# Pooled softmax scalars in PSUM, all SBUF splits on GpSimd, a first pass of 320 tokens and a new order table, in a fused attention and feed-forward kernel

## The chip, the cores and the metric

One core of a Trainium2 chip runs the whole program. The metric is device time in microseconds of one execution. The engines are TensorE (PE, with its weight loads as PEld), VectorE (DVE), ScalarE (ACT), GpSimd (POOL) and SyncE (SP), whose queue issues nearly all DMAs.

## The reference

Eight batches of eight heads, 576 positions, head size 64. Attention is the sum of two parts: a pooled softmax over means of four positions, repeated four times, and a softmax over a band of seven neighbours. The result goes through a feed-forward layer.

```python
q_d = q.reshape(B, H, Sd, factor, D).mean(axis=3)      # the same for k, v
out_d = sm_attn(q_d, k_d, v_d)
out_up = np.repeat(out_d, factor, axis=2)
mask = np.abs(pos[:, None] - pos[None, :]) < factor
scores = np.where(mask, scale * q @ k^T, -1e9)
out_local = softmax(scores) @ v
x = (out_up + out_local).transpose(0, 2, 1, 3).reshape(B * S, H * D)   # 4608 x 512
h = x @ w_in                                            # w_in 512 x 2048
out = np.maximum(0.01 * h, h) @ w_out                   # w_out 2048 x 512
```

## The kernel before

**Feed-forward.** The 4608 tokens are cut into twelve chunks: the first batch into 256 and 320 tokens, the other seven batches into ten chunks of 256 to 512 (`plan`). A float32 factor is held as a high part (rounded to the fp32r type) and a low part (the rest), and each product is three matmuls: high by high, high by low, low by high. `w_in` and `w_out` are cut into 16 blocks f. Of each chunk the up-projection makes one PSUM bank per f (line 1169, 12 matmuls), `leaky` (lines 1259 to 1263) applies the activation on ScalarE twice and takes the low part `gl` on VectorE, and the down-projection adds it to four accumulator banks (line 1298, 12 matmuls for each f). The passes are: chunk 0 over f 0 to 7, chunk 1 over all f, chunk 0 over f 8 to 15, and then the other chunks.

**Weights** come in 64-bit floats and are joined to float32 in `convert`: a cast on ScalarE (line 405), a join on VectorE (407), the high part on VectorE or ScalarE (420, 424), the low part on GpSimd (427). In the first pass this goes on while TensorE already multiplies.

**Fast products.** The last four chunks have 512 tokens and use seven products in place of eight half-size ones for two blocks f (`products`, line 1199). Their seven operands T0 to T6 are sums of the quarters of x and come from `operands`: `split` copies an operand's high part on ScalarE (504) and takes its low part (507), on GpSimd for T1 and T5 and on VectorE for the other five; `less` (514) makes the sums on VectorE. x lies in SBUF (`stage`, `hmem`), the sums in PSUM (`pt`).

**Attention.** Batch 0 goes through TensorE: `pooled`, and `banded` in windows of 64 queries, in two stretches (`BLKS`), one for chunk 0 and one for chunk 1. For batches 1 to 7, GpSimd multiplies (lines 990 and 1054), VectorE sums (997, 1061), and TensorE only transposes; the pooled part runs in `pair`, twice for each batch, 14 times in all. A `pair` scores on TensorE into two banks (line 779), takes the maxima on VectorE into a small SBUF tile `st` (785), scales them there (787), lets ScalarE exponentiate and sum into `st` (793), turns the sums into factors (798, 800, VectorE) and multiplies by them (805, ScalarE).

```python
nc.vector.tensor_scalar(out=st[:, :, 0], in0=st[:, :, 0], scalar1=-SCALE / (FAC * FAC), ...)   # 787
nc.vector.tensor_scalar(out=rc, in0=rc, scalar1=1e-9, scalar2=float(FAC), ...)                 # 798, rc = st[:, :, 1]
(nc.vector if eng == "DVE" else nc.gpsimd).tensor_tensor(out=lo, in0=x, in1=hi..., op=subtract) # 507
```

**Order.** Every engine runs its instructions in the order in which the program has issued them. `Order.run` sets it: each task (a `pair`, a weight, a chunk) has a rank, and the instruction that could start first by a table of costs goes next, ties by rank. `SHIFTS` moves the ranks of single tasks. The banks are eight: two `hp` for the up-projection, four accumulators, and `pt0` and `pt1`, which all the rest shares.

Of the kernel before, what the change touches and what calls it, by code (L numbers as in the profile page):

```python
# [13 lines left out]
ALU = mybir.AluOpType  # L14
AX = mybir.AxisListType
PSUM = bass.MemoryType.PSUM

B, H, S, D = 8, 8, 576, 64
DE = D + 1
FAC = 4  # L20
SD = S // FAC
# [11 lines left out]
FSPLIT = 8  # L33
BANDED = 1
WIN = 64 + W - 1
BLKS = ((0, 4), (4, 9))
HALFS = 4
HEADS = 2
HF = NF // 2
# [4 lines left out]
HN = 256  # L44
# [2 lines left out]

def plan():

    chunks, at = [(0, 256, ()), (256, 320, ())], S  # L50
    parts = {b: [] for b in range(BANDED, B)}
    g = 0
    for i, n in enumerate(SIZES):
        mine, z = [], g + n
        while g < z:
            b, j = divmod(g, BLK)
            room = min(BLK - j, z - g)
            m = -(-room // -(-room // MAXSEG))
            mine.append((b + BANDED, j, j + m, (g - z + n) * NBLK))
            parts[b + BANDED].append((i + 2, j, j + m, (g - z + n) * NBLK))  # L60
            g += m
        chunks.append((at, n * NBLK, tuple(mine)))
        at += n * NBLK
    assert g == (B - BANDED) * BLK
    return chunks, parts
# [6 lines left out]
def pieces(j0, j1):  # L72
# [13 lines left out]
RATE = 270e3  # L86
SAFE = 0.4
SHIFTS = {
# [23 lines left out]
}  # L112
POLICIES = [SHIFTS]
HP, PT = ("hp0", "hp1"), ("pt0", "pt1")
# [166 lines left out]
def attn_moe(policy, ctx, tc, qkt, vd, vs3, qkb, vb, vwb, band, identb, w_in, w_out, ident, out, sums):  # L281
# [207 lines left out]
    def operands(i):  # L489
        tx = yield from wait(("x", i), LANDED[i])  # L490
        (b11, t1), (b21, b22) = ([x[:, :, :HN], x[:, :, HN:]] for x in xt[i])

        def taken(s):
            if i == FIRST:
                t = yield from wait(("up", LAST[2])) if s == 6 else wait(("emptied", bank_of(s)))
            h = yield from slot(f"t{s}")
            if i == FIRST:
                h.t = t
            return h

        def split(s, h, x, t, own=True):
            hi, lo = put(i, s)
            t = yield from op("ACT", 2 * HN, t, h.t)
            nc.scalar.copy(out=hi, in_=x)
            eng = "POOL" if s in (1, 5) else "DVE"
            t = yield from op(eng, 2 * HN, t, port=own)
            (nc.vector if eng == "DVE" else nc.gpsimd).tensor_tensor(out=lo, in0=x, in1=hi.bitcast(F32), op=ALU.subtract)
            od.signal(("T", i, s), t)
            ready[i, s] = h
            return t  # L510

        def less(out, x, y, *after, port=False):
            t = yield from op("DVE", 2 * HN, *after, port=port)
            nc.vector.tensor_tensor(out=out, in0=x, in1=y, op=ALU.subtract)
            return t

        h = yield from taken(0)
        yield from split(0, h, b11, tx)
        s_2, s_3 = yield from two(*PT)
        h = yield from taken(2)  # L520
        yield from split(2, h, t1, tx)
        t2 = bank(s_2).rearrange("p (c m) -> p c m", c=2)
        t = yield from less(t2, b22, t1, tx, s_2.t, port=True)
        h = yield from taken(3)
        tv = yield from split(3, h, t2, t, False)
        t3 = bank(s_3).rearrange("p (c m) -> p c m", c=2)
        tt = yield from less(t3, t2, b11, t, s_3.t)
        h = yield from taken(1)
        yield from split(1, h, b21, tx)
        h = yield from taken(4)  # L530
        s_3.free((yield from split(4, h, t3, tt, False)))
        h = yield from taken(5)
        tb = yield from split(5, h, b22, tx)
        t = yield from less(t2, b21, t2, tv, tt)
        h = yield from taken(6)
        t = yield from split(6, h, t2, t, False)
        s_2.free(t)
        return max(t, tb)
# [204 lines left out]
    def pair(b, u):  # L743
# [36 lines left out]
                                     qk_d[i][rows, SD:2 * SD], start=True, stop=True)  # L780
        for s in s_qds:
            s.free(t)
        for p in range(2):
            t = yield from op("DVE", 432, t, s_st.t)
            nc.vector.tensor_reduce(out=st[:, p, 0], in_=scs[p][:, :3 * SD].rearrange("p (a s) -> p a s", a=3), axis=AX.X, op=ALU.max)
        t = yield from op("DVE", 6, t)
        nc.vector.tensor_scalar(out=st[:, :, 0], in0=st[:, :, 0], scalar1=-SCALE / (FAC * FAC), scalar2=None, op0=ALU.mult)  # L787
        for p in range(2):
            t = yield from op("ACT", 432, t, s_pd.t, times=8)
            sc = scs[p]  # L790
            for qi in range(3):
                o = pds[:, qi, :, p, :QB]
                nc.scalar.activation(out=o, in_=like(sc[:, qi * SD:(qi + 1) * SD], o), func=AF.Exp, scale=SCALE / (FAC * FAC),
                                     bias=st[:, p, 0, qi:qi + 1], accum_out=st[:, p, 1, qi:qi + 1])
            s_bs[p].free(t)
        t = yield from op("DVE", 6, t)
        rc = st[:, :, 1]
        nc.vector.tensor_scalar(out=rc, in0=rc, scalar1=1e-9, scalar2=float(FAC), op0=ALU.add, op1=ALU.mult)  # L798
        t = yield from op("DVE", 6, t)
        nc.vector.reciprocal(out=rc, in_=rc)  # L800
        ts = [t, t]
# [670 lines left out]
```

## Time and profile before

| what | value |
|---|---|
| median of 3 runs | 923.71 us (922.93 to 927.31) |
| the profiled execution's own time | 923.97 us |
| its span in the profile | 921.8 us (2.1 us lie around it) |
| TensorE busy | 891.0 us, 97% of the span |
| weight loads | 827.5 us, 90% |
| VectorE, GpSimd, ScalarE | 664.1, 590.2 and 472.3 us (72%, 64%, 51%) |
| granted TensorE clock, mean | 0.991 |
| the chain that ended last | TensorE 84%, VectorE 7%, DMA 4%, ScalarE 2% |

Busy time is the time in which an engine has an instruction running. The chain that ended last is followed back from the last instruction, at each step to what released it. TensorE is the engine that is nearly always at work, so time is found where it is not: at the start, in a few gaps, at the end, and where its clock is granted at half.

### The profile page before, as it was taken

To read this page: it belongs to the slowest core of one execution; us is meant where nothing else is said; L and a number is where in the kernel's file an instruction comes from. 1 tells how busy PE (TensorE), PEld (TensorE's weight loads), DVE (VectorE), ACT (ScalarE), POOL (GpSimd) and SP (SyncE) were. 2 spreads that over 40 slices of the span, in tenths; PEclk is the share of its full clock that TensorE was granted. 3 is DMA by queue.
4 is the path that set the end of the run, shared out by engine and by line. 5 is a ranking of instruction groups with operands and counts; after the bars stand their busy time and mean duration, and the time that the engine had idled before them with its cause. 6 is when DMAs were issued, how large, how long until landed. Compare 5 with 4: busy or idle time off the path is not lost.

```text
span 921.8 us, 17665 instructions
## 1 busy us (share of the span) xinstructions
PE 891.0 (97%) x6549; PEld 827.5 (90%) x6549; DVE 664.1 (72%) x1027; ACT 472.3 (51%) x1443; POOL 590.2 (64%) x301
## 2 busy tenths in 40 slices
PE   5889999999999999999999999999999999999998
PEld 3778999999999989999999998888898888989986
DVE  5777799779788987887978789787866776232221
ACT  4668465454546446556445355554745464335332
POOL 4565887888878675847898887877676786000000
PEclk9799999999999999999999999999999999999999
DMA  9788646655435644756645627576675464315321
GB/s 256 251 262 306 211 138 210 189 163 190 158 111 180 224 133 136 268 171 198 184 159 192 224 85 265 194 268 221 206 268 193 153 218 165 125 58 160 116 92 46
DMA packets 70069, 169.21 MB, mean 184 GB/s; under 512 B 7952, under 2 KB 21008, under 8 KB 69984
## 3 DMA queue, kind: packets, MB, share of 16 engines
q1 hardware_dynamic: 69840, 167.96, 55.7%
q8 instruction: 51, 0.84, 0.4%
q14 instruction: 34, 0.28, 0.1%
q10 hardware_dynamic: 144, 0.13, 0.0%
HBM read 149.71 MB, written 18.35 MB: 182 GB/s over the span
## 4 chain that ended last, share of the span: by engine, by line
PE 84%; DVE 7%; DMA 4%; ACT 2%; issue 1%; POOL 1%; SPq 0%; POOLq 0%; DVEq 0%; ACTq 0%
PE acc L1298 39%; PE hp L1169 23%; PE hp L1199 8%; PE pt L1199 7%; PE pt L1100 1%; PE pt L826 1%; PE pt L812 1%; PE pt L779 1%; DMA prod<-in_w_out_dram 1%; DVE xloc L1061 1%; DMA v<-in_vb_dram 1%; DVE st_p L798 1%; DVE gl L1263 1%; DMA r<-sums 1%; DVE st_p L787 1%
## 5 line engine op out<-in xcount | busy, mean ns | idle before, releaser
L1054 POOL TENSOR_TENSOR prod<-v,s 128x896 f32<-128x896 f32 (+2 forms) x104 | 264.2, 2543 | 50.6 <-DVE xloc L1061 29.1
L990 POOL TENSOR_TENSOR prod<-k 128x910 f32<-128x910 f32 (+2 forms) x104 | 250.4, 2411 | 67.8 <-DVE s L997 49.7
L1298 PE MATMUL acc<-gh,w 128*128 128x320 f32 (+3 forms) x704 | 193.0, 336 | 0.0
L1259 ACT ACTIVATE gh<-hp 128x320 fp32r<-128x320 f32 (+3 forms) x155 | 72.4, 467 | 135.3 <-PE acc L1298 116.2
L1061 DVE TENSOR_REDUCE xloc<-prod 128x128 f32<-128x896 f32 (+2 forms) x104 | 132.4, 1273 | 6.6 <-POOL prod L1054 6.6
L997 DVE TENSOR_REDUCE s<-prod 128x14 f32<-128x910 f32 (+2 forms) x104 | 133.9, 1288 | 3.1 <-POOL prod L990 3.0
L1298 PEld LDWEIGHTS acc<-gh,w 128*128 128x128 f32 x704 | 124.9, 189 | 7.5 <-issue 0.8
L1169 PE MATMUL hp<-xh,w 128*128 128x320 f32 (+2 forms) x512 | 125.5, 316 | 3.2 <-DVE gl L1263 3.2
L1298 PE MATMUL acc<-gh,woh 128*128 128x320 f32 (+3 forms) x352 | 118.8, 337 | 0.0
L1298 PE MATMUL acc<-gl,w 128*128 128x320 f32 (+3 forms) x352 | 117.3, 333 | 1.1 <-DVE gl L1263 1.1
L1298 PE MATMUL acc<-gl,woh 128*128 128x320 f32 (+3 forms) x352 | 117.0, 332 | 0.8 <-DVE gl L1263 0.7
L1298 PE MATMUL acc<-gh,wol 128*128 128x320 f32 (+3 forms) x352 | 116.9, 332 | 0.0
L1263 DVE TENSOR_TENSOR gl<-hp,gh 128x320 fp32r<-128x320 f32 (+3 forms) x155 | 80.4, 519 | 45.9 <-ACT hp L1260 45.1
L1169 PEld LDWEIGHTS hp<-xh,w 128*128 128x128 f32 x512 | 89.1, 189 | 5.1 <-DVE gl L1263 4.0
L1169 PE MATMUL hp<-xl,w 128*128 128x320 f32 (+2 forms) x256 | 79.5, 311 | 0.0
L1260 ACT ACTIVATE hp<-hp 128x320 f32<-128x320 f32 (+3 forms) x165 | 77.5, 470 | 0.3
L1298 PEld LDWEIGHTS acc<-gh,wol 128*128 128x128 f32 x352 | 66.1, 188 | 4.4
L1298 PEld LDWEIGHTS acc<-gl,w 128*128 128x128 f32 x352 | 66.5, 189 | 3.9 <-DVE gl L1263 1.4
L1298 PEld LDWEIGHTS acc<-gh,woh 128*128 128x128 f32 x352 | 66.2, 188 | 2.7 <-issue 1.0
L1298 PEld LDWEIGHTS acc<-gl,woh 128*128 128x128 f32 x352 | 66.2, 188 | 2.4 <-DVE gl L1263 1.2
L1169 PE MATMUL hp<-xh,w_even 128*128 128x320 f32 (+2 forms) x256 | 65.6, 322 | 0.9 <-DVE gl L1263 0.9
L1169 PEld LDWEIGHTS hp<-xl,w 128*128 128x128 f32 x256 | 48.5, 189 | 0.0
(300 smaller groups left out, 1855.3 us busy)
## 6 DMA issues: line engine op xcount, KB each, us to landing
r<-sums SPq DMA_DIRECT2D x64, 512.0 KB, 3.5
k<-in_qkb_dram SPq DMA_DIRECT2D x48, 390.0 KB, 3.7
qk<-in_qkt_dram SPq DMA_DIRECT2D x32, 576.0 KB, 5.3
k<-in_qkb_dram SPq DMA_DIRECT2D x52, 325.0 KB, 4.7
v<-in_vb_dram SPq DMA_DIRECT2D x48, 288.0 KB, 3.4
v<-in_vb_dram SPq DMA_DIRECT2D x52, 256.0 KB, 3.6
qk<-in_vs_dram SPq DMA_DIRECT2D x28, 384.0 KB, 4.2
out_dram<-o SPq DMA_DIRECT2D x37, 128.0 KB, 3.8
```

The costliest lines, as they stand in the source:

```text
L779: nc.tensor.matmul(scs[p][outs, qi * SD:(qi + 1) * SD], qk_d[i][rows, qi * QB:qi * QB + 64], qk_d[i][rows, SD:2 * SD], start=True, stop=True)
L787: nc.vector.tensor_scalar(out=st[:, :, 0], in0=st[:, :, 0], scalar1=-SCALE / (FAC * FAC), scalar2=None, op0=ALU.mult)
L990: nc.gpsimd.tensor_tensor(out=prv, in0=view(half(s_k), 0, [[DE, nj], [1, DE]]).unsqueeze(2).to_broadcast([128, nj, W, DE]), in1=view(half( ...
L997: nc.vector.tensor_reduce(out=s[:, 2 * u + p, :nj], in_=prv, axis=AX.X, op=ALU.add)
L1054: nc.gpsimd.tensor_tensor(out=prv, in0=view(half(s_v), 0, [[1, nj], [nv, D], [1, W]]), in1=s[:, p, :nj].unsqueeze(2).to_broadcast([128, nj ...
L1061: nc.vector.tensor_reduce(out=xl_t[:, :nj, p], in_=prv, axis=AX.X, op=ALU.add)
L1169: nc.tensor.matmul(hp[:, :n], column_of(wt, c), column(x, c), start=k == 0, stop=k == 3 * NC - 1)
L1199: nc.tensor.matmul(out, a[c], b[:, c], start=first and c + k == 0, stop=c == 1 and k == 2, skip_group_check=True)
L1259: nc.scalar.activation(out=gh, in_=like_of(hp[:, :n], s_g), func=AF.Prelu, alpha=0.01)
L1260: nc.scalar.activation(out=hp[:, :n], in_=hp[:, :n], func=AF.Prelu, alpha=0.01)
L1263: nc.vector.tensor_tensor(out=gl, in0=hp[:, :n], in1=gh.bitcast(F32), op=ALU.subtract)
L1298: nc.tensor.matmul(acc[:, :n] if len(g.shape) == 2 else acc.rearrange("p (k m) -> p k m", k=2), wt[:, es], g, start=f == f0 and j == 0, st ...
```

## The change

Four edits and a new table.

1. **Pooled softmax scalars** (`pair`): the maxima go to spare columns of the first score bank (`top`), ScalarE's sums too (`rest`), and the two small VectorE instructions read PSUM and write `st`. The first bank is freed after the second half's exponentials and the sums' step, no longer after its own exponentials.
2. **Low parts** (`split`): all four operands that lie in SBUF (T0, T1, T2, T5) are split on GpSimd; before, two of them.
3. **One sum of x**: for `b22 - t1` ScalarE first copies `b22` to PSUM, and VectorE then subtracts `t1` there.
4. **First pass**: chunk 0 has 320 tokens, chunk 1 has 256; `BLKS` follows (five windows, then four).
5. **`SHIFTS`** has other numbers throughout.

```diff
-BLKS = ((0, 4), (4, 9))
+BLKS = ((0, 5), (5, 9))
-    chunks, at = [(0, 256, ()), (256, 320, ())], S
+    chunks, at = [(0, 320, ()), (320, 256, ())], S
...
-    20: -40, 21: 10.7, 23: 9.9, 24: 6.5, 25: -55.1, 26: 21.1, 27: -8.2, 28: 1.6, 29: -25, 30: 14.4, 31: -134.7, 32: -21.1, 33: -15.5, 34:
+    22: 3.2, 23: -5.5, 25: -10.3, 26: 13.7, 27: -32.4, 29: -3.2, 30: -24.7, 31: -86.8, 32: -59.2, 33: 0.8, 34: -76.4, 35: 28.7, 36: -2, 38:
...
-            eng = "POOL" if s in (1, 5) else "DVE"
-            t = yield from op(eng, 2 * HN, t, port=own)
+            eng = "POOL" if own else "DVE"
+            t = yield from op(eng, 2 * HN, t)
...
-        t = yield from less(t2, b22, t1, tx, s_2.t, port=True)
+        t = yield from op("ACT", 2 * HN, tx, s_2.t)
+        nc.scalar.copy(out=t2, in_=b22)
+        t = yield from less(t2, t2, t1, t)
...
+        top, rest = (scs[0][:, 3 * SD + 8 * k:3 * SD + 8 * k + 6].rearrange("q (p a) -> q p a", p=2) for k in range(2))
         for p in range(2):
             t = yield from op("DVE", 432, t, s_st.t)
-            nc.vector.tensor_reduce(out=st[:, p, 0], in_=scs[p][:, :3 * SD].rearrange("p (a s) -> p a s", a=3), axis=AX.X, op=ALU.max)
+            nc.vector.tensor_reduce(out=top[:, p], in_=scs[p][:, :3 * SD].rearrange("p (a s) -> p a s", a=3), axis=AX.X, op=ALU.max)
         t = yield from op("DVE", 6, t)
-        nc.vector.tensor_scalar(out=st[:, :, 0], in0=st[:, :, 0], scalar1=-SCALE / (FAC * FAC), scalar2=None, op0=ALU.mult)
+        nc.vector.tensor_scalar(out=st[:, :, 0], in0=top, scalar1=-SCALE / (FAC * FAC), scalar2=None, op0=ALU.mult)
...
-                                     bias=st[:, p, 0, qi:qi + 1], accum_out=st[:, p, 1, qi:qi + 1])
-            s_bs[p].free(t)
+                                     bias=st[:, p, 0, qi:qi + 1], accum_out=rest[:, p, qi:qi + 1])
+            if p:
+                s_bs[p].free(t)
         t = yield from op("DVE", 6, t)
         rc = st[:, :, 1]
-        nc.vector.tensor_scalar(out=rc, in0=rc, scalar1=1e-9, scalar2=float(FAC), op0=ALU.add, op1=ALU.mult)
+        nc.vector.tensor_scalar(out=rc, in0=rest, scalar1=1e-9, scalar2=float(FAC), op0=ALU.add, op1=ALU.mult)
+        s_bs[0].free(t)
```

Lines of the changed program are two to five higher (507 stays, 944 becomes 949, 1169 becomes 1174). Of the new order three places are shown.

**DMA queue, start.** SyncE's first loads from the second batch-0 head pair on. `qk` are queries and keys of a pair of heads, `su_vs` and `su_vw` their values (or, from `vwb`, windows of values); the rest are weight blocks. Before:

```order
L324 DMA qk_92<-in_qkt_dram 128x1152
L324 DMA su_vs<-in_vd_dram 72x1024
L324 DMA su_vs<-in_vwb_dram 70x640
L324 DMA qk_95<-in_qkt_dram 128x1152
L324 DMA su_vs<-in_vd_dram 72x1024
L324 DMA k<-in_w_out_dram 128x2048
L324 DMA v<-in_w_in_dram 128x2048
L324 DMA su_vw<-in_vwb_dram 70x512
L324 DMA qk_180<-in_qkt_dram 128x1152
```

The change:

```order
L324 DMA qk_92<-in_qkt_dram 128x1152
L324 DMA su_vs<-in_vd_dram 72x1024
L324 DMA k<-in_w_out_dram 128x2048
L324 DMA qk_94<-in_qkt_dram 128x1152
L324 DMA su_vs<-in_vd_dram 72x1024
L324 DMA su_vw<-in_vwb_dram 70x640
L324 DMA qk_97<-in_qkt_dram 128x1152
```

The fourth pair's `qk` has one weight block ahead of it where it had two.

**ScalarE, end of the start.** The last instructions up to the copy of the fourth part of x's high half (`xh`, line 944 and now 949), on which the first up-projection waits. `hmem` is the cast of a weight block. Before:

```order
L424 CAST w_odd<-stage 128x256
L897 ACTIVATE xloc<-xloc 128x350
L405 CAST hmem<-k 128x512
L690 COPY outd<-acc_470 128x144
L901 ACTIVATE lst<-lst 128x5
L405 CAST hmem<-xl_104 128x512
L944 CAST xh_90<-hp_487 128x256
```

The change:

```order
L405 CAST hmem<-xl_105 128x512
L906 ACTIVATE lst<-lst 128x4
L920 COPY su_pt<-pt_490 70x384
L920 COPY su_pt<-pt_503 70x256
L405 CAST hmem<-k 128x512
L424 CAST w_even<-xl_105 128x512
L405 CAST hmem<-v 128x512
L405 CAST hmem<-prod 128x512
L949 CAST xh_90<-acc_509 128x320
```

Ahead of that copy there are now ten casts of weight blocks (line 405) and five roundings (line 424), where there were eight and three.

**GpSimd, first set of fast-product operands.** `xl` and `xh` are what the low parts are written to, `prod` the multiplications of the banded attention. Before, T1 and T5 only:

```order
L1054 TENSOR_TENSOR prod<-v,s 128x1344
L990 TENSOR_TENSOR prod<-k 128x910
L1019 TENSOR_TENSOR s<-s,st_l 128x84
L507 TENSOR_TENSOR xl_6189<-hmem,xh_6188 128x512
L1054 TENSOR_TENSOR prod<-v,s 128x1344
L507 TENSOR_TENSOR xl_7014<-hmem,xl_7014 128x512
```

The change:

```order
L995 TENSOR_TENSOR prod<-k 128x910
L507 TENSOR_TENSOR xh_6148<-stage,xh_6148 128x512
L507 TENSOR_TENSOR xl_6149<-stage,xl_6149 128x512
L1059 TENSOR_TENSOR prod<-v,s 128x1344
L507 TENSOR_TENSOR xl_6149<-hmem,xh_6148 128x512
L507 TENSOR_TENSOR xl_7018<-hmem,xl_7018 128x512
```

T0 and T2, which were on VectorE, stand in GpSimd's queue behind a multiplication and ahead of the next one.

## Rows read from the trace of the kernel before

**Rows 1.** The profile's page: the span, and TensorE's busy time.

```profile
span 921.8 us, 17665 instructions
...
PE 891.0 (97%) x6549; PEld 827.5 (90%) x6549; DVE 664.1 (72%) x1027; ACT 472.3 (51%) x1443; POOL 590.2 (64%) x301
```

**Rows 2.** Windows: stretch, us, busy us (instructions) per engine, granted clock, DMA.

```profile
0.00:40.00 40.00, 26.46 (x294) 19.59 (x294) 25.90 (x60) 22.32 (x70) 21.09 (x27) 0.89 0.89 268
...
40.00:80.00 40.00, 34.52 (x349) 31.12 (x346) 29.29 (x59) 26.85 (x70) 18.97 (x19) 0.93 0.68 229
...
151.00:342.00 191.00, 186.88 (x1465) 182.33 (x1464) 163.13 (x238) 97.50 (x334) 151.65 (x64) 1.00 0.54 174
...
560.00:735.00 175.00, 172.82 (x1204) 152.02 (x1204) 135.09 (x204) 95.55 (x290) 129.69 (x63) 1.00 0.67 224
```

**Rows 3.** Timeline of TensorE after 100 us: start, length, work, idle before.

```profile
157.81 0.39 PE L1169 MATMUL hp<-xh,w 128*128 128x256 f32 x1 [0.99 <-DVE gl L1263]
...
225.73 0.41 PE L1169 MATMUL hp<-xh,w_even 128*128 128x320 f32 x1 [0.94 <-DVE gl L1263]
...
341.38 0.45 PE L1169 MATMUL hp<-xh,w 128*128 128x384 f32 x1 [1.96 <-DVE gl L1263]
...
554.48 0.44 PE L1298 MATMUL acc<-gl,w 128*128 128x384 f32 x1 [1.08 <-DVE gl L1263]
...
734.68 0.98 PE L1199 MATMUL hp<-xl,r 128*128 128x256 f32 x6 [1.49 <-DVE hp L1213]
```

**Rows 4.** Timelines of GpSimd and VectorE, at 222 and 730 us.

```profile
222.19 3.06 POOL L1054 TENSOR_TENSOR prod<-v,s 128x1344 f32<-128x1344 f32 x1
...
222.72 2.56 DVE L787 TENSOR_SCALAR st_p<-st_p 128x6 f32<-128x6 f32 x1
...
730.09 3.58 DVE L507 TENSOR_TENSOR xl<-stage,xl 128x512 fp32r<-128x512 f32 x1
```

**Rows 5.** Groups by line, VectorE: count | busy us, mean ns | idle before.

```profile
L787 DVE TENSOR_SCALAR st_p<-st_p 128x6 f32<-128x6 f32 x14 | 12.0, 859 | 0.2
...
L798 DVE TENSOR_SCALAR st_p<-st_p 128x6 f32<-128x6 f32 x14 | 15.8, 1132 | 0.0
```

**Rows 6.** Lines 787 and 507: instructions, min/median/max ns, first to last start us.

```profile
L787 DVE TENSOR_SCALAR st_p<-st_p x14: 154/524/2561, 68.4 to 694.6; 128x6 f32<-128x6 f32 x14
...
L507 DVE TENSOR_TENSOR xl<-stage,xl x4: 683/2056/3583, 551.4 to 823.9; 128x512 fp32r<-128x512 f32 x4
...
L507 POOL TENSOR_TENSOR xl<-hmem,xh x4: 1294/1301/1317, 555.2 to 826.4; 128x512 fp32r<-128x512 f32 x4
```

**Rows 7.** Timelines of GpSimd and VectorE at 17 us: the first batch.

```profile
16.91 0.67 POOL L652 TENSOR_TENSOR qk_d<-su_half 128x288 f32<-128x288 f32 x1
...
17.36 0.16 DVE L727 TENSOR_SCALAR st_d<-acc 128x3 f32<-128x3 f32 x1 [1.38 <-ACT su_pd L720]
```

**Rows 8.** Window behind the gap at 341 us, columns as in rows 2.

```profile
341.40:344.70 3.30, 3.30 (x12) 3.30 (x13) 3.20 (x8) 2.09 (x7) 2.21 (x1) 0.62 0.30 92
```

**Rows 9.** Timeline of TensorE: first up-projection, last gap before 100 us.

```profile
40.10 0.58 PE L1169 MATMUL hp<-xh,w_even 128*128 128x256 f32 x1
...
79.71 0.41 PE L1169 MATMUL hp<-xh,r 128*128 128x320 f32 x1 [1.92 <-DVE gl L1263]
```

**Rows 10.** Groups by line, ScalarE (first: before 80 us), columns as in rows 5.

```profile
L405 ACT CAST hmem<-prod 128x512 f16<-128x512 bf16 x6 | 4.5, 774 | 3.2 <-DMA prod<-in_w_out_dram 3.2
...
L793 ACT ACTIVATE pds<-pt,st_p 128x144 f32<-128x144 f32 x84 | 30.9, 388 | 15.6 <-DVE st_p L787 15.6
...
L793 ACT ACTIVATION_READ_ACCUMULATOR pds<-pt,st_p 128x1 f32 x84 | 17.9, 213 | 0.0
```

**Rows 11.** The chain of waits: start, length, work, instructions merged.

```profile
91.75 1.76 PE hp L1169 x12
...
173.03 1.42 PE hp L1169 x12
...
902.10 16.07 PE acc L1298 x69
```

44 rows, old and new, of the table SHIFTS are left out of this document.

## The prediction

> **What bounds the kernel now.** I read the page first, then the windows, then the gaps of TensorE, and last what runs on the other engines at those gaps. The page says that TensorE has work for 891.0 of 921.8 us [rows 1]. The change leaves the number of its matmuls and their columns as they are (the first batch is 256 + 320 tokens before and 320 + 256 after), so the time can only move by what TensorE loses: idle time, and time at the lower clock. The windows show where [rows 2] (the columns: the stretch, its length, busy us of PE, PEld, DVE, ACT and POOL, the granted clock, DMA share and GB/s). Up to 40 us it does little but the first batch's attention. From 40 to 80 us it is busy for 34.52 of 40 us, at a mean clock of 0.93: 5.5 us idle and, as 0.07 of 40 us, 2.8 us of clock, 8.3 us lost in all. From 80 to 151 us it loses nothing. From 151 to 342 us it idles 4.1 us, from 560 to 735 us 2.2 us. After 905 us comes the tail, which the change does not touch.
>
> The gaps after 100 us are few [rows 3] (in brackets stand the idle time before the row and who ended it). Five are longer than 0.9 us: 0.99, 0.94, 1.96, 1.08 and 1.49, together 6.46 us, and VectorE ends each of them. What held VectorE is seen in its timeline. At 222.72 us line 787, six elements in each partition, takes 2.56 us and ends at 225.28; the multiplication on GpSimd that had started just before ends at 222.19 + 3.06 = 225.25 [rows 4]. The `gl` that TensorE waits for at 225.73 stands behind it in VectorE's queue. At 730.09 us line 507, with both inputs in SBUF, takes 3.58 us. The same two lines at other moments take 0.15 and 0.68 us [rows 6]. So a short VectorE instruction of these kinds waits until a running GpSimd instruction ends. Lines 787 and 798 run 14 times each and cost 12.0 and 15.8 us of VectorE [rows 5]. In the timeline the gaps at 157, 225 and 341 us have one of these two just ahead of the late `gl`; those at 554 and 734 us have a line 507. [...]
>
> **The change, part by part.**
>
> *Softmax scalars in PSUM.* Lines 787 and 798 now read PSUM. The nearest row is the same step in the first batch, which already reads PSUM: 0.16 us, at 17.36 us, while GpSimd was at work from 16.91 to 17.58 [rows 7]. So 28 instructions go from 27.8 to 28 x 0.16 = 4.5 us, 23.3 us of VectorE freed, most of it off the path. On the path lie the three gaps that they cause, 0.99 + 0.94 + 1.96, and the clock behind the third, 1.25: 5.14 us. [...]
>
> *Splits on GpSimd, one copy on ScalarE.* VectorE loses the eight line-507 instructions on `stage` (up to 3.58 us each), and its first subtraction gets an input in PSUM. GpSimd gets eight at 1.30 us [rows 6], 10.4 us in all, in a stretch where it is busy 129.69 of 175 us [rows 2]. ScalarE gets four copies, each bounded by the 0.77 us of line 405 on as many elements [rows 10], and is about half busy. On the path lie the gaps 1.08 + 1.49 = 2.57 us.
>
> *Sum of the two:* 5.14 + 2.57 = 7.7 us can go. What is late next is the `gl` itself, behind VectorE's sums of 1 to 1.5 us, and the new places of GpSimd's splits; for these I put 1.2 us back, one average gap, and take **6.5 us**. The ends: 7.7 if nothing follows, and 3.9 if only the three gaps of 787 and 798 go and the clock loss comes elsewhere.
>
> *The first pass.* The first up-projection starts at 40.10 us [rows 9] and waits for the fourth part of x. Two things move it. The fourth pair's queries and keys have one weight block less ahead in the DMA queue: 0.52 MB at 268 GB/s [rows 2] is 2.0 us earlier at best. ScalarE has two more casts (405) and two more roundings (424) ahead of the last copy of x, 4 x 0.774 us [rows 10] = 3.1 us later, and all five windows of a quarter more width stand in that chain: up to 8% of VectorE's 25.90 us [rows 2], an estimate of 2 us. So the start lies between 2.0 us earlier and 5.1 later; I take 3.1 later, since in the new order three of these casts and a rounding are the last ScalarE instructions before the copy. On the other side the first pass has more work for each weight that arrives: 12 matmuls of 320 columns take 1.76 us, of 256 columns 1.42 [rows 11], so 16 such groups (eight blocks, up and down) hold 5.4 us more work, taken from a pass that loses nothing. It can fill the 8.3 us lost between 40 and 80. The 1.92 us before 79.71 [rows 9] are one such gap: ScalarE's queue waits for a late weight block. I take half, 4.2 us. Together **1.1 us** gained; the ends are 7.4 gained (2.0 + 5.4) and 5.1 lost.
>
> *Nothing* for the rest: eight more output transfers of 160 columns, hidden behind hundreds of us of TensorE work, and the same tail.
>
> **The sum.** The profiled execution took 923.97 us, 0.26 above the median of the runs. 923.97 - 6.5 - 1.1 - 0.26 = **916.1 us** on the scale of the median.
>
> **Rivals.** A measurement of this kernel can tell about 0.5% from no change: 919.1 and 928.3 us are the borders.
>
> - *The first pass fills everything*: the start does not move and all 8.3 us go: 923.7 - 6.5 - 8.3 = 908.9. For it: DMA is busy 0.89 of the first 40 us but only 0.68 of the next 40, so loads could keep pace. Against it: ScalarE's longer queue.
> - *The start eats the gain*: 5.1 us later and nothing filled, since in that stretch ScalarE's casts feed TensorE: 923.7 - 6.5 + 5.1 = 922.3.
> - *Slower: the first score bank.* `pt0` and `pt1` serve all transposes, maxima and products' operands. The first bank is now held through the second half's exponentials and the sums: 3 x (0.388 + 0.213) us of line 793 [rows 10] + 0.16 = 1.96 us more, 14 times. If TensorE waits for it each time, that is 27 us. It decides from the seventh pair on: 919.1 is passed early, and (928.3 - 916.1) / 1.96 = 6.2 waits make it slower than before by over 0.5%; nine give 933.7. Against it: none of the five gaps is ended by a release of a bank.
> - *T0 and T2 late on GpSimd.* A split now may stand behind a multiplication of 3.06 us [rows 4]. If this shows at two of the four changes of chunk: 916.1 + 6.1 = 922.2. Against it: at the shortest of these changes the new order has 27 down-projection matmuls of 512 columns (16.07 / 69 = 0.233 us each) and 30 of 256 (1.42 / 12 = 0.118) [rows 11] between the last use of the old T0 and the first of the new: 9.8 us, while the cast, one multiplication and the split need 0.8 + 3.1 + 1.3 = 5.2.
> - *It does not do what it says*: the small instructions wait for GpSimd even when they read PSUM, and other VectorE work takes the place of line 507: only the first pass moves, 922.6. Against it: the 0.16 us beside a running GpSimd instruction [rows 7]. [...]
>
> **How the numbers follow.** Forecast 0.50, with a range of its own of 912 to 919. First pass fills everything 0.15. Start eats the gain 0.15. Bank 0.10. Late T0 0.06. No effect 0.04. Faster by over 0.5%: the first two, 0.65. Within 0.5%: start, T0 and no effect, 0.25. Slower: 0.10. The range of 909 to 924 takes in all but the bank and the lowest part of the filled first pass.
>
> **What would show it.** Right: the successors of lines 787 and 798 at 0.16 us each time, no line 507 on VectorE above 0.7 us, no gap of TensorE above 0.9 us between 150 and 800 us, no half clock after 100 us, the first up-projection at 42 to 45 us and fewer than 5 us lost in the 40 us behind it. Wrong: gaps ended by a bank's release or by GpSimd's splits, a first up-projection beyond 46 us with gaps behind it, or new gaps behind VectorE's long sums.

## The result, and the profile after

The changed kernel takes **913.36 us** (median of six runs, 911.55 to 915.02); the kernel before, beside it, 923.32 (919.46 to 932.59). The ratio is 0.9877, with a 95% interval of 0.983 to 0.9923: faster, by 1.2%. Here and below a ratio weighs all runs, so it lies by the means (913.2 to 924.7 us here) and not by the medians, whose ratio is 0.9892. The forecast was 916.1 in a range of 909 to 924.

The page of the changed kernel, where [rows 1] stand before:

```profile
span 911.7 us, 17700 instructions
...
PE 889.9 (98%) x6549; PEld 826.2 (91%) x6549; DVE 630.0 (69%) x1023; ACT 477.4 (52%) x1447; POOL 601.1 (66%) x309
...
PE 91%; DVE 4%; DMA 2%; ACT 1%; POOL 1%; issue 1%; DVEq 0%; POOLq 0%; ACTq 0%
```

The span is 10.1 us shorter, while TensorE's busy time moves by 1.1 us. VectorE lost 34 us of busy time: 23.3 as the prediction had it for the pairs' scalars and 14.2 with the eight splits, while 3.4 came back on other lines. In the chain that ended last, TensorE's share rose from 84% to 91% and VectorE's fell from 7% to 4%.

The windows, columns as in [rows 2]:

```profile
40.00:80.00 40.00, 38.90 (x363) 35.31 (x363) 33.45 (x65) 29.74 (x80) 22.68 (x22) 0.93 0.79 273
80.00:151.00 71.00, 68.26 (x596) 66.08 (x595) 55.00 (x79) 40.72 (x119) 55.69 (x32) 0.98 0.60 189
151.00:342.00 191.00, 191.00 (x1456) 187.72 (x1449) 155.66 (x247) 96.47 (x323) 156.56 (x67) 1.00 0.54 173
...
560.00:735.00 175.00, 174.52 (x1224) 153.00 (x1224) 126.24 (x202) 97.43 (x287) 132.24 (x69) 1.00 0.69 226
```

From 151 to 342 us the 4.12 us of idle time are gone, from 560 to 735 us 1.7 of 2.2. From 40 to 80 us TensorE is busy 4.4 us more. But between 80 and 151 us, where the kernel before lost nothing, it now idles 2.74 us. The gaps, in TensorE's timeline (in brackets the idle time before the row, and who ended it):

```profile
44.32 0.61 PE L1174 MATMUL hp<-xh,w_even 128*128 128x320 f32 x1
...
93.39 0.58 PE L1303 MATMUL acc<-gh,woh 128*128 128x256 f32 x1 [2.47 <-ACT o L1347]
...
503.04 0.44 PE L1174 MATMUL hp<-xh,r 128*128 128x384 f32 x1 [0.56 <-DVE gl L1268]
578.66 0.39 PE L1204 MATMUL pt<-xh,w_even 128*128 128x256 f32 x1 [0.27 <-ACT mix L1213]
```

The five gaps of [rows 3] are gone; nothing after 100 us is longer than 0.56 us. One new gap stands at 93 us. The instructions that the change moved, by line (count, then min/median/max ns):

```profile
L790 DVE TENSOR_SCALAR st_p<-pt x14: 156/166/168, 71.0 to 698.9; 128x6 f32<-128x6 f32 x14
...
L802 DVE TENSOR_SCALAR st_p<-pt x14: 150/155/165, 75.2 to 702.1; 128x6 f32<-128x6 f32 x14
...
L507 POOL TENSOR_TENSOR xh<-stage,xh x4: 1284/1290/1296, 537.2 to 800.2; 128x512 fp32r<-128x512 f32 x4
...
L507 DVE TENSOR_TENSOR xh<-pt,xh x4: 642/686/692, 542.4 to 815.2; 128x512 fp32r<-128x512 f32 x4
```

L790 and L802 are the lines 787 and 798 of before [rows 5, 6]: 0.16 us every time, where they took up to 2.56 and 2.92. No line 507 on VectorE is over 0.7 us. Line 798 in the kernel before, which no row shows:

```profile
L798 DVE TENSOR_SCALAR st_p<-st_p x14: 153/964/2923, 72.8 to 699.9; 128x6 f32<-128x6 f32 x14
```

**The new gap at 93 us.** GpSimd, VectorE and ScalarE in the timeline ahead of it, and the window of lower clock behind it:

```profile
87.36 4.42 POOL L995 TENSOR_TENSOR prod<-k 128x910 f32<-128x910 f32 x2
...
88.14 4.19 DVE L407 SCALAR_TENSOR_TENSOR w<-w,hmem 128x512 int32<-128x512 int32 x2 [0.26 <-ACT hmem L405]
...
92.37 0.66 ACT L424 CAST w<-w 128x512 fp32r<-128x512 f32 x1 [1.75 <-DVE w L407]
...
93.05 0.88 ACT L1347 COPY o<-acc 128x160 f32<-128x160 f32 x4
...
93.30:96.70 3.40, 3.31 (x15) 3.31 (x16) 2.60 (x4) 2.59 (x8) 1.45 (x2) 0.50 0.83 250
```

Read it from the end. TensorE waits for an output copy (L1347) that empties an accumulator. That copy stands in ScalarE's queue behind the rounding of a late weight (L424), which waits for VectorE's join of that weight (L407). Two joins take 4.19 us; at other places one takes 0.68. GpSimd's two products begin 0.8 us before the first of them and end 0.6 us before the last. It is the wait of [rows 4] once more, at a line that the change left alone and the prediction did not list. It costs 2.47 us, and from 93.3 to 96.7 us the clock is granted at 0.50: half of 3.4 us, 1.7 us more. In the kernel before, too, two joins of this line were held up, where TensorE lost nothing by it:

```profile
79.90 3.55 DVE L407 SCALAR_TENSOR_TENSOR w<-w,hmem 128x512 int32<-128x512 int32 x2
```

### The profile page after: what moved, and what is told of

Same layout as the page of the kernel before. It is cut to its first block, busy times and chain, and to the rows that moved or that the text cites. A ratio compares the mean times of both kernels' runs of the same rounds, so it can differ in the third digit from the quotient of the medians.

```text
span 911.7 us, 17700 instructions
## 1 busy us (share of the span) xinstructions
PE 889.9 (98%) x6549; PEld 826.2 (91%) x6549; DVE 630.0 (69%) x1023; ACT 477.4 (52%) x1447; POOL 601.1 (66%) x309
## 4 chain that ended last, share of the span: by engine, by line
PE 91%; DVE 4%; DMA 2%; ACT 1%; POOL 1%; issue 1%; DVEq 0%; POOLq 0%; ACTq 0%
PE acc L1303 43%; PE hp L1174 23%; PE hp L1204 10%; PE pt L1204 7%; PE pt L1105 1%; PE pt L817 1%; PE pt L781 1%; PE pt L831 1%; DMA qk<-in_qkt_dram 1%; DMA out_dram<-o 1%; DVE w L407 1%; DVE gl L1268 0%; DVE s L1002 0%; POOL su_pd L672 0%; PE pt L932 0%
## 5 line engine op out<-in xcount | busy, mean ns | idle before, releaser
L1264 ACT ACTIVATE gh<-hp 128x320 fp32r<-128x320 f32 (+3 forms) x158 | 74.4, 471 | 143.9 <-PE acc L1303 119.1
L1268 DVE TENSOR_TENSOR gl<-hp,gh 128x320 fp32r<-128x320 f32 (+3 forms) x158 | 82.6, 524 | 60.0 <-ACT hp L1265 59.2
L1174 PE MATMUL hp<-xh,w_even 128*128 128x320 f32 (+2 forms) x256 | 63.5, 314 | 0.2 <-DVE gl L1268 0.2
```

The lines of the kernel that those rows point to most:

```text
L1174: nc.tensor.matmul(hp[:, :n], column_of(wt, c), column(x, c), start=k == 0, stop=k == 3 * NC - 1)
L1264: nc.scalar.activation(out=gh, in_=like_of(hp[:, :n], s_g), func=AF.Prelu, alpha=0.01)
L1268: nc.vector.tensor_tensor(out=gl, in0=hp[:, :n], in1=gh.bitcast(F32), op=ALU.subtract)
```

## The experiments

Theory 1: the time comes from the waits for GpSimd that are gone; the first pass and the new order about break even. The rival: the new order and the first pass bring it, and the waits were mostly hidden. The kernels ran in three groups of four, each with runs of the kernel before on its chip: 925.7 us beside e0, e1, e2 and e10; 922.26 beside e11, e13, f1 and f2; 924.76 beside e0b, f2b, f3 and e14. A ratio is always to the kernel before of the same group.

**The changed kernel again** (e0).

> The changed kernel once more, to have it beside the next three on one chip. Both theories: 911.5 to 915 us, the ratio to the kernel before 0.986 to 0.991, one gap of TensorE over 0.9 us behind 60 us (2.5 us at 93 us), no other up to the tail.

Measured: 913.17 us, ratio 0.9867 (0.9841 to 0.9892), the 2.47 us gap again at 93.37, no other over 0.3 us behind it.

**Scalars back in SBUF** (e1), every engine's order as in the changed kernel.

```diff
-        top, rest = (scs[0][:, 3 * SD + 8 * k:3 * SD + 8 * k + 6].rearrange("q (p a) -> q p a", p=2) for k in range(2))
+        top, rest = st[:, :, 0], st[:, :, 1]
```

> The changed kernel with the pairs' maxima and sums in SBUF again, every engine's instructions in the same order. Theory 1 (the gain is the port waits of the pairs' small operations): L790 and L802 take 0.15 to 2.6 us again instead of 0.16, together over 12 us more of VectorE, gaps of TensorE of 0.9 to 2 us come back in the banded passes (80 to 560 us), and the time is 3 to 6 us above the changed kernel of this call, some 917 us. Rival (the gain comes from the new order and the first pass, the waits were hidden): VectorE is busier by the same, but the time is within 1.5 us of the changed kernel and no new gap over 0.9 us shows.

Measured: 917.13 us, 4.0 above e0; ratio 0.9905 (0.9878 to 0.9932). Its lines, and one of its gaps with what stood on VectorE:

```profile
L790 DVE TENSOR_SCALAR st_p<-st_p x14: 161/490/2804, 70.7 to 699.0; 128x6 f32<-128x6 f32 x14
...
L802 DVE TENSOR_SCALAR st_p<-st_p x14: 154/1264/2748, 75.0 to 703.0; 128x6 f32<-128x6 f32 x14
...
703.02 2.75 DVE L802 TENSOR_SCALAR st_p<-st_p 128x6 f32<-128x6 f32 x1 [0.28 <-ACT pds L796]
...
706.92 0.97 PE L1204 MATMUL pt<-xh,w 128*128 128x256 f32 x6 [1.33 <-DVE s L1014]
```

VectorE is 19.7 us busier (649.4 against 629.7). TensorE's gaps that come back are 0.53, 0.44 and 1.33 us, at 356, 534 and 707 us; in the first two, again, one of these lines stands ahead of the late `gl`. Theory 1 holds, though only one gap is over 0.9 us. What it calls port waits shows as a wait for GpSimd, and the trace does not say over what: this L802 ends at 705.77 us, GpSimd's product beside it (2.91 us from 702.82) at 705.73. The gaps add up to 2.3 us; the profiled execution, at 915.09 the shortest of the six, had no half clock behind 93 us (last section), which would be another 1.7 of the 4.0 us if the other five had it; no trace shows that.

**T0 and T2 back on VectorE** (e2), in the same places.

```diff
-            (nc.vector if eng == "DVE" else nc.gpsimd).tensor_tensor(out=lo, in0=x, in1=hi.bitcast(F32), op=ALU.subtract)
+            (nc.gpsimd if s in (1, 5) else nc.vector).tensor_tensor(out=lo, in0=x, in1=hi.bitcast(F32), op=ALU.subtract)
```

> The changed kernel with the low parts of the splits T0 and T2 (two SBUF inputs) on VectorE again, in the same places of the order. Theory 1: these subtractions last 0.7 to 3.6 us instead of 1.3 on GpSimd, and where GpSimd runs a long product TensorE waits 1 to 1.5 us in two of the late passes; time 1 to 3 us above the changed kernel. Rival (T0 and T2 have slack in the new order): within 0.7 us, no new gap over 0.9 us behind 100 us.

Measured: 919.7 us, 6.5 above e0; ratio 0.993 (0.9904 to 0.9955). One group of line 507, the gaps, and VectorE ahead of the last:

```profile
L507 DVE TENSOR_TENSOR xh<-stage,xh x4: 680/1468/3385, 540.7 to 806.6; 128x512 fp32r<-128x512 f32 x4
...
727.27 2.25 DVE L507 TENSOR_TENSOR xh<-stage,xh 128x512 fp32r<-128x512 f32 x1
...
563.78 0.72 PE L1303 MATMUL acc<-w,woh 128*128 128x512 f32 x2 [0.70 <-ACT o L1347]
...
647.15 0.97 PE L1204 MATMUL hp<-xh,r 128*128 128x256 f32 x6 [1.51 <-ACT hp L1213]
...
731.64 0.97 PE L1204 MATMUL hp<-w,w 128*128 128x256 f32 x6 [1.69 <-DVE hp L1218]
```

Direction as theory 1 has it, size not: twice as much as expected. 3.9 us are these gaps, and 1.7 us the start of this execution (its first pass began at 46.0 us, that of e0 at 44.3). These eight instructions put 10.3 us on VectorE and cost more than the pairs' 28, which put 19.7 us on it: here it counted where a wait stands, not how much of it there is.

**The order of before, without the waits** (e10). First pass, offsets and order are those of the kernel before. The operation on the sums becomes a reduction over four copies of each: it gives four times the sum, without the added 1e-9. `b22 - t1` keeps its two SBUF inputs.

```diff
-            (nc.vector if eng == "DVE" else nc.gpsimd).tensor_tensor(out=lo, in0=x, in1=hi.bitcast(F32), op=ALU.subtract)
+            (nc.vector if s in (3, 4, 6) else nc.gpsimd).tensor_tensor(out=lo, in0=x, in1=hi.bitcast(F32), op=ALU.subtract)
...
+        top = scs[0][:, 3 * SD:3 * SD + 6].rearrange("q (p a) -> q p a", p=2)
...
-            nc.vector.tensor_reduce(out=st[:, p, 0], in_=scs[p][:, :3 * SD].rearrange("p (a s) -> p a s", a=3), axis=AX.X, op=ALU.max)
+            nc.vector.tensor_reduce(out=top[:, p], in_=scs[p][:, :3 * SD].rearrange("p (a s) -> p a s", a=3), axis=AX.X, op=ALU.max)
...
-        nc.vector.tensor_scalar(out=st[:, :, 0], in0=st[:, :, 0], scalar1=-SCALE / (FAC * FAC), scalar2=None, op0=ALU.mult)
+        nc.vector.tensor_scalar(out=st[:, :, 0], in0=top, scalar1=-SCALE / (FAC * FAC), scalar2=None, op0=ALU.mult)
...
-        nc.vector.tensor_scalar(out=rc, in0=rc, scalar1=1e-9, scalar2=float(FAC), op0=ALU.add, op1=ALU.mult)
+        nc.vector.tensor_reduce(out=st[:, :, 0], in_=rc.unsqueeze(3).to_broadcast([128, 2, 3, FAC]), axis=AX.X, op=ALU.add)
...
-        nc.vector.reciprocal(out=rc, in_=rc)
+        nc.vector.reciprocal(out=rc, in_=st[:, :, 0])
```

> The kernel before, its first pass, offsets and order on every engine kept, with the waits for GpSimd taken out: the maxima go to spare PSUM columns, the operation on the sums becomes a reduction (it gives four times the sum and leaves out the 1e-9 added to it), and the low parts of T0 and T2 run on GpSimd. Theory 1 (the waits alone are the late part of the gain): the gaps of 0.9 to 2 us at 157, 225, 341, 554 and 734 us are gone, the time is 4 to 7.7 us under the kernel before, ratio 0.992 to 0.996, that is 917 to 920 us. Rival (the new order is what gains): other work is late instead, the time is within 1.5 us of the kernel before.

Measured: 913.06 us (910.33 to 917.48), ratio 0.9868 (0.9836 to 0.9899): as fast as e0. Its windows:

```profile
151.00:342.00 191.00, 191.00 (x1527) 187.38 (x1526) 155.65 (x245) 99.89 (x345) 156.32 (x67) 1.00 0.56 179
342.00:545.00 203.00, 203.00 (x1462) 199.13 (x1461) 162.79 (x264) 104.84 (x351) 160.42 (x73) 1.00 0.57 185
545.00:735.00 190.00, 190.00 (x1328) 169.04 (x1327) 143.11 (x222) 106.02 (x315) 153.35 (x80) 1.00 0.67 221
735.00:905.00 170.00, 170.00 (x1068) 151.72 (x1067) 59.97 (x98) 71.09 (x181) 36.33 (x17) 1.00 0.37 120
```

From 151 us to the tail TensorE never idles. Theory 1 stands, and even its range (917 to 920) was too small: without the waits the old order gains all that the whole change gains. The median moved by 12.6 us, the profiled execution (917.48, the longest of the six) by 6.5. This execution idled 3.27 us at 83 us, with half clock from 82.4 to 89.2 us, and the trace of before lost nothing between 80 and 151 us; what the other five lost there is not recorded. Two by-products. The subtraction left with two SBUF inputs still takes up to 1.98 us and opens no gap: the copy by ScalarE (edit 3) is worth nothing that shows here. And the reduction from SBUF to SBUF, which stands where line 798 stood, does not wait, though 12 of the 14 lie wholly within a running GpSimd product:

```profile
L799 DVE TENSOR_REDUCE st_p<-st_p x14: 168/170/174, 75.1 to 695.1; 128x6 f32<-128x24 f32 x14
```

**The new order with the waits** (e11): the edits of e1 and e2 together.

> The changed kernel's first pass, offsets and order on every engine, with both waits for GpSimd put back (pairs' scalars in SBUF, low parts of T0 and T2 on VectorE; ScalarE's copy of x stays): what the first pass and the new order are worth alone. Theory 1 (the waits are the whole late gain, and start and order come out even): the losses of 4.0 and 6.5 us add up, some 921 to 925 us, ratio to the kernel before 0.995 to 1.002. Rival (first pass and order gain a part of their own, and the waits' removal is worth less with the new order): 915 to 919 us, ratio under 0.994.

Measured: 921.06 us, ratio 0.9977 (0.9959 to 0.9995). So four cells, in ratios:

| | waits in | waits out |
|---|---|---|
| first pass 256, old order | 1 | 0.9868 |
| first pass 320, new order | 0.9977 | 0.9877 |

Taking the waits out is worth 1.3% in the old order and 1.0% in the new one; first pass and table together (they were not tried apart) are worth 0.2% with the waits and nothing without. The rival falls.

**One edit at a time in the old order** (e13: the line-507 edit of e10 alone; e14: the other edits of e10 alone).

> The kernel before with one edit: the low parts of T0 and T2 on GpSimd, in the same places of the order; the pairs' scalars stay in SBUF. Theory 1: TensorE's gaps at 554, 557 and 734 us (1.08, 0.71 and 1.49 us) go, those at 157, 225 and 341 us stay; 3 to 4.5 us under the kernel before. Rival (the pairs' waits alone carry the gain, or GpSimd is late with T0 and T2): within 1 us, with new gaps in the late passes.

> The kernel before with the pairs' waits alone taken out (maxima in spare PSUM columns, the operation on the sums as a reduction that gives four times the sum and leaves out the added 1e-9); the low parts of T0 and T2 stay on VectorE. Theory 1: the gaps at 157, 225, 267 and 341 us (0.99, 0.94, 0.24, 1.96 us, and the half-clock stretch behind the last, 1.25 us) go, those at 554 to 735 us stay; 4.5 to 6.5 us under the kernel before. Rival (the two waits hide each other, so that either alone brings nearly all or nearly nothing): under 2 us or over 8 us.

Measured: e13 917.84 us, 4.4 under before, ratio 0.9946 (0.9924 to 0.9968). e14 915.78, 9.0 under, ratio 0.9913 (0.9878 to 0.9947, which is 4.9 to 11.3 us). Windows of e13:

```profile
151.00:342.00 191.00, 186.93 (x1463) 182.37 (x1462) 163.22 (x241) 97.49 (x333) 152.41 (x65) 1.00 0.54 174
545.00:735.00 190.00, 190.00 (x1310) 168.90 (x1311) 146.97 (x219) 106.32 (x316) 152.98 (x78) 1.00 0.66 222
```

and of e14:

```profile
151.00:342.00 191.00, 191.00 (x1503) 187.78 (x1504) 156.61 (x248) 100.42 (x346) 156.29 (x67) 1.00 0.56 178
545.00:735.00 190.00, 185.99 (x1280) 164.26 (x1280) 148.07 (x223) 103.65 (x307) 142.40 (x71) 1.00 0.65 220
```

Each edit fills one stretch and leaves the other: the splits bring 3.97 us behind 545 us, the scalars 4.12 us before 342 us. The kernel before in the later stretch:

```profile
545.00:735.00 190.00, 186.03 (x1299) 163.85 (x1297) 150.03 (x219) 102.69 (x308) 141.21 (x69) 1.00 0.64 214
```

In the trace the two are apart, as theory 1 says. The median of e14, 9.0 us under, is beyond what theory 1 expected (4.5 to 6.5) and within what its rival did (over 8); the interval holds both, so here the trace decides and not the time.

**Taking away the gap at 93 us** (f1: the rounding of that one weight on VectorE; f3: on GpSimd).

```diff
-                nc.scalar.copy(out=h, in_=x)
+                (nc.vector.tensor_copy if f == 10 else nc.scalar.copy)(out=h, in_=x)
```

> The changed kernel with one instruction moved: the rounding of one late weight (the one of the 11th slice of the up-projection) goes from ScalarE to VectorE, in the same place of the plan, so that the four output copies behind it on ScalarE don't wait for VectorE's L407, which stands behind GpSimd's products. Theory 1: the 2.47 us gap at 93 us falls under 0.5 us and the half-clock stretch behind it (3.4 us long) goes: 2.5 to 4.2 us under the changed kernel, some 909 to 911 us. Rival (the accumulators are held by something else too, or the pass behind is short of weights): the gap moves by less than 10 us and the time is within 1 us.

> The changed kernel with the rounding of the same late weight as in the last call on GpSimd instead of ScalarE (there it went to VectorE and the gap at 93 us came back as 1.52 and 0.86 us at 96 and 103 us). Theory 1 (VectorE itself, busy with L407 behind GpSimd's products and two long reductions, is late for the next pass): gaps of 0.8 to 1.2 us at 96 us and some 0.9 us at 103 us stay, 0.5 to 1.5 us under the changed kernel. Rival (only the one rounding was late): both gaps go, 2.5 to 4 us under the changed kernel.

Measured: f1 912.62 us, ratio 0.9893 (0.987 to 0.9916); f3 912.43, ratio 0.9869 (0.984 to 0.9898), 2.2 under the changed kernel of its group (914.64, e0b below). VectorE and TensorE of f1 behind 93 us:

```profile
93.30 0.54 DVE L424 CAST w<-w 128x512 fp32r<-128x512 f32 x1
93.75 1.34 DVE L758 TENSOR_REDUCE qk_d<-qk 128x288 f32<-128x1152 f32 x1
95.02 1.08 DVE L1002 TENSOR_REDUCE s<-prod 128x14 f32<-128x910 f32 x1
96.03 0.41 DVE L1268 TENSOR_TENSOR gl<-hp,gh 128x256 fp32r<-128x256 f32 x1
...
96.49 0.38 PE L1174 MATMUL hp<-xh,r 128*128 128x256 f32 x1 [1.52 <-DVE gl L1268]
102.56 0.39 PE L1174 MATMUL hp<-xh,r 128*128 128x256 f32 x1 [0.86 <-DVE gl L1268]
```

The chain through ScalarE was read rightly: the gap at 93 us is gone, and no half clock follows (1.00 granted from 96.5 to 99.9 us). But 2.4 us of gaps come back a few us later, since VectorE, late by the two joins, has two long reductions ahead of the next `gl`. With the rounding on GpSimd (f3) they are 1.08 and 0.99 us, as its theory 1 had them, and again no half clock follows (1.00 over 80 to 151 us): 2.47 + 1.7 - 2.07 = 2.1 us, which is the 2.2 measured, more than the 0.5 to 1.5 expected. The expected 2.5 to 4.2 us of f1 were a miss; its rival describes it better. No run of the changed kernel stands in the group of f1, so its gain, if any, is not shown.

**A kernel without that gap** (f2): e10, with one decoding cast on GpSimd. In the order of before the stretch around 80 us has a gap of its own, 1.92 us [rows 9], behind a cast that waits in ScalarE's queue for its load, ahead of the activation's two instructions (GELU in the text below). What e10 changes on the sums, f2 changes too.

```diff
-        nc.scalar.copy(out=head.bitcast(F16).rearrange("p (m h) -> p m h", h=2)[:, :, 1], in_=top)
+        (nc.gpsimd.tensor_copy if (f, k) == (10, 0) else nc.scalar.copy)(out=head.bitcast(F16).rearrange("p (m h) -> p m h", h=2)[:, :, 1], in_=top)
```

> The kernel before with both waits for GpSimd taken out as in the last call, and one ScalarE copy of the weight decoding (11th slice, up-projection), which waited for its load ahead of two GELU instructions, on GpSimd instead. Theory 1 (the gap of 1.9 to 3.3 us at 80 to 83 us is that late load in ScalarE's in-order queue): the gap is gone, 2 to 5 us under the kernel without the waits (913.1), 908 to 911 us. Rival (GpSimd's own queue then waits for the load, and the weights behind it come late): a gap of over 1 us between 80 and 110 us stays, and the time is 912 to 916 us.

> The kernel before with the waits taken out and the late weight copy on GpSimd, again, to set it against the changed kernel on one chip. Theory 1 (the waits were all that the change took away in net, and the load at 80 us is a loss of the old first pass alone): 1 to 3 us under the changed kernel of this call. Rival (the two are even): within 1 us of it.

> The changed kernel a third time, beside the next three on one chip: 912 to 915 us.

Measured: f2 911.94 us, ratio 0.9882 (0.9856 to 0.9908). In the last group f2 took 911.12 (909.28 to 913.16), ratio 0.9857 (0.9826 to 0.9888), and the changed kernel 914.64 (913.82 to 915.55), ratio 0.9898 (0.9866 to 0.993): 3.5 us apart, with no run in common. That is a little beyond the 1 to 3 us of theory 1. e10 at the gap (ScalarE, TensorE, window):

```profile
81.65 0.76 ACT L405 CAST hmem<-w 128x512 f16<-128x512 bf16 x1 [2.39 <-DMA w<-in_w_in_dram]
...
83.44 0.64 PE L1170 MATMUL hp<-xh,r 128*128 128x320 f32 x1 [3.27 <-DVE gl L1264]
...
83.40:86.90 3.50, 3.46 (x13) 3.47 (x14) 3.50 (x3) 3.15 (x9) 3.34 (x3) 0.50 1.04 423
```

and f2 (GpSimd, window):

```profile
78.61 0.78 POOL L405 CAST hmem<-w 128x512 f16<-128x512 bf16 x1 [11.21 <-DMA w<-in_w_in_dram]
...
80.00:151.00 71.00, 71.00 (x575) 69.25 (x574) 62.83 (x80) 42.52 (x128) 62.77 (x35) 1.00 0.64 218
```

The cast now waits for its load on GpSimd, which has nothing urgent there, and TensorE loses nothing from 80 to 151 us. Whether that gap cost e10 time in the median is not shown: by ratio f2 (0.9882 and 0.9857) can't be told from e10 (0.9868), which ran in another group, and 911.94 us lies just between the ranges of theory 1 and its rival. With the old first pass and the old table f2 has the lowest median of the study; f3 beside it (911.2 to 912.69) overlaps with it, the changed kernel does not.

## Why the prediction was right, point by point

The verdict was right and the time 2.7 us too high. The steps:

- **What held VectorE: right.** The lines 787, 798 and 507 wait for a running GpSimd instruction; put back they wait again (up to 2.80 and 2.75 us in e1, 3.39 in e2), taken out of the old order the gaps go (e10). Those that waited have no one form: line 407, with two SBUF inputs, took 4.19 us for two, line 507, with two also, up to 3.58 us; lines 787 and 798, with one input, in SBUF, up to 2.56 and 2.92 us. The reduction of e10, from SBUF too, took at most 0.174 us. From PSUM the pairs' two lines took at most 0.168 us, so the rival "does not do what it says" falls.
- **Scalars, 0.16 us each and 5.14 us of path: right, the path 0.7 us low.** 0.150 to 0.168 us, each time. In the old order 4.12 us of idle time go (e14), with the 0.24 us gap at 267 us that was not listed. The clock, put at 1.25 us (0.38 of the 3.3 us of [rows 8]), was 1.7: that window ends at 344.7 us, the stretch granted at 0.50 only at 345.5 (last section). It was not sure to be there: in e13 the same gap was followed by 1.00. Reading PSUM adds nothing that shows: L790 takes 0.156 us at the least from PSUM, and 0.161 from SBUF in e1.
- **Splits, 2.57 us: mis-sized.** The trace has 3.97 us. The step took only the two gaps above 0.9 us; the smaller ones in that stretch went with the same edit alone (e13), though one of 0.32 us at 620 us had been ended by a DMA.
- **1.2 us put back for what is late next: near in size, by luck.** In the old order nothing was late next (e10). In the new one 1.45 us of idle time are left from 151 to 905 us, but a late `gl` is only 0.56 of them, in one gap that e0 does not have. Of before's 8.09 us of idle time there and 1.7 us of clock, 8.3 are gained, where the sum had 6.5.
- **The first pass, 1.1 us: the net near, by luck.** The start came 4.2 us later (44.32 against 40.10), within the 42 to 45 named, where the sum had 3.1. In the 40 us behind it TensorE lost 1.0 us (0.4 idle, 0.6 of clock) of the 8.3 lost before: it filled nearly all, where the step took half. By difference the lead at 80 us is 6.2 us: 10.1 of span, less 8.3 from behind 151 us, and the 4.4 us (2.74 idle, 1.7 of clock) lost between. At 151 us 1.8 us of the lead are left, where the sum had 1.1.
- **"Nothing for the rest ... hidden": the step that failed.** The first pass's output copies were not hidden. They stand in ScalarE's queue behind a rounding that waits for GpSimd by way of VectorE, and gave back 2.47 + 1.7 = 4.2 us. The price was in reach: line 407 has two SBUF inputs like line 507, and two joins take 3.55 us at 79.90 us in the kernel before, at a place where it cost nothing.
- **Rivals.** No gap is ended by a bank's release for a pair, so the slower rival has nothing. T0 and T2 were not late on GpSimd. "No half clock after 100 us" held; it came at 93.3 (0.50 up to 96.7).

TensorE from 151 to 905 us, in the kernel before and in the changed one:

```profile
151.00:905.00 754.00, 745.91 (x5284) 697.13 (x5283) 544.95 (x825) 378.45 (x1176) 489.02 (x223) 1.00 0.54 177
...
151.00:905.00 754.00, 752.55 (x5305) 702.94 (x5298) 514.03 (x826) 383.70 (x1181) 500.64 (x232) 1.00 0.55 177
```

In sum: 1.4 us more from the splits and 0.7 from the scalars, less 0.2 for what was left, and 0.6 from the first 151 us make the 2.5 us by which the trace beat the sum. What stays open is why the medians of e2, e10 and e14 moved by 2.6 to 3.2 us more than the gaps between 151 and 905 us and the 1.7 us of clock explain (6.5 against 3.9, 12.6 against 9.8, 9.0 against 5.8): single executions differ before 100 us, and only one of each has a trace.

## What to carry to other kernels

List the waiting instructions by what they have in common (here two SBUF inputs, up to 3.58 us, or a `tensor_scalar` from SBUF to SBUF, up to 2.92 us, beside a busy GpSimd), not by the lines that the change touches: here the next one on the list gave 4.2 us back. Count all gaps of a stretch that have the same cause, the short ones too, and read a loss of clock to where the lower level ends (345.5 us here, where the window read ended at 344.7). And before a new order or tiling is credited with a gain, put the mechanism's edits alone into the old order: here they carried all of it.

## What the runs showed of the hardware

- **A small reduction from SBUF to SBUF (0.170 us) does not wait for GpSimd** where the `tensor_scalar` in its place (line 798) took up to 2.92 us, so moving the operand to PSUM is not the only way out.
- **The clock behind a gap of some 2 us is not fixed.** The kernel before had 1.96 us of idle time at 341 us [rows 3]; the 0.62 of [rows 8] is 0.99 up to 342.2 us and 0.50 behind that:

```profile
342.20:345.55 3.35, 3.35 (x12) 3.35 (x12) 3.25 (x8) 1.58 (x5) 3.05 (x1) 0.50 0.22 82
```

In e13 the same gap was followed by a granted clock of 1.00:

```profile
340.09 0.44 PE L1169 MATMUL hp<-xh,w 128*128 128x384 f32 x1 [1.95 <-DVE gl L1263]
...
340.10:343.50 3.40, 3.40 (x19) 3.40 (x20) 3.30 (x9) 2.19 (x7) 2.31 (x1) 1.00 0.30 89
```

Behind the 2.47 us at 93 us the granted clock was 0.50 from 93.3 to 96.7 us in the changed kernel, and in e1, with the same gap, 1.00:

```profile
93.33:96.80 3.47, 3.47 (x28) 3.29 (x29) 3.28 (x5) 2.88 (x9) 1.36 (x2) 1.00 0.77 236
```

In e10 it was 0.50 from within the gap of 3.27 us on, to 89.2 us. A loss of clock that one trace shows is thus not a fixed part of a gap's price.
- **The late load at 80 us differs from run to run.** The gap behind it was 1.92, 3.27, 1.51 and 3.57 us in four kernels that share the order up to there (before, e10, e13, e14). The new order has no such gap, and the changed kernel's runs lie closer together: 912.55 to 915.0 in e0, against 920.75 to 929.34 for the kernel before of that group. The runs of f2, where ScalarE no longer waits for that load, span 4.8 and 3.9 us, those of e10 7.2; six runs each don't settle whether the load is the cause.
- **ScalarE's read-out of its sum is shorter into PSUM.** `ACTIVATION_READ_ACCUMULATOR` takes 0.164 us (median of 84) in the changed kernel, where the sums go to PSUM, 0.210 in e1 and 0.212 in the kernel before, where they go to SBUF.
